# Gated products cut into pieces of 293 columns, differences moved to GpSimd, weight sums and end loads moved in a fused attention and gated feed-forward kernel

## The chip, the cores and the metric

One core of one Trainium2 chip runs the whole program. Its engines are TensorE (PE: matmuls; its weight loads are listed as PEld), VectorE (DVE), ScalarE (ACT), GpSimd (POOL) and SyncE (SP, which here only issues DMAs). The metric is the device time of one execution in microseconds (us); smaller is better.

## The reference, cut to what matters

```python
# x: 2048 x 512, 32 heads of 16, F = 1792
g = sigmoid((x * gate_w).sum(-1, keepdims=True))
q, k, v = heads of x @ wqkv
a = softmax(q @ k.T / 4) @ v  @ wo                     # attention
b = (sigmoid(x @ w_gate) * (x @ w_up)) @ w_down        # gated linear unit
out = g * a + (1 - g) * b
```

## The kernel before, in words

**Main loop.** 256 periods, two steps of 128 keys by 1024 queries each. A period holds 8 score matmuls (L679), each followed by an exponential on ScalarE (L681); 8 matmuls whose largest values a later pair of heads needs (L293), each followed by a maximum over its 512 columns on VectorE (L295, "reduce" below); 12 groups of dense matmuls (L164: gate, up and later query and key weights, in high and low halves); and 16 value matmuls (L953). The period is named by the number k in `values(k)`, and V is the start of its value matmuls. The strings `STEADY` (periods 0 to 244) and `LAST` (from 245, without reduces) are the order on TensorE.

**What sets the order of the rest.** `plans(k, kind, step)` puts a step into period k: "load" steps at its start (DMAs on SP's queue), "pool" steps into the list `later`, "act" steps before `values(k)`, "dve" steps right behind it, which is behind the period's 8th reduce. `work` lets GpSimd work off the lists, for about 2 us in mid period and 2.6 us at its end. In mid period GpSimd also passes a token (`turn`, L175) that TensorE's next dense group waits for. GpSimd's standing work is the dense products' partial sums (L541: `chain`, `had`, `side`), a sum of value products per period (L970) and the splits of weights into halves (L138, L141).

**Gated products.** `plan_quad(i, c, k0)` takes four 128 x 512 tiles of gate (`hg`) and up (`hu`), makes tanh on ScalarE (L725), `(tanh + 1) * up` on VectorE (`gated`, L737) and four differences T1 to T4 (`minus`, L740), and stores seven tiles in `op_d`. A quad takes 8 periods, and there are 13; the 14th is `last_quad` in the end. Before, k0 is 139 + 16i + 8c; the four whole-tile products fall in periods k0 + 3, 5, 7, 10, T1 and T2 on VectorE in k0 + 6 and 8, T3 and T4 on GpSimd in k0 + 10 and 11.

**Weight sums and denominators.** `plan_combos` forms sums of blocks of `w_down` on GpSimd (four additions of 128 x 256 each) for seven f. `denominators` loads softmax sums as 32 rows of 512, takes the reciprocal in pieces on VectorE (L910), multiplies by the gate (L912) and stores them in `rec_d`.

**End.** 98 units of six matmuls (two halves, seven products `PRODUCTS`, seven f; L1252) use a stored tile `op`, split by ScalarE (L103) and VectorE (L106), with up to nine tiles loaded ahead (L875); between them come 132 matmuls of the attention output (L151), whose inputs `heads_split` multiplies by the denominators (L1142), and the weights of later products (`weights_at`).

Of the kernel before, what the change touches and what calls it, by code (L numbers as in the profile page):

```python
# [45 lines left out]
def gated_mix(ctx, tc, x, xT, wqk, wv, wo, w_gate, w_up, w_down, gate_w, out):  # L46
# [28 lines left out]
    g_d = dram.tile([2, NS, 4, 32], F32, name="g_d")  # L75
    wc_d = dram.tile([2, HF, P, 2, 256], F32, name="wc_d")
# [13 lines left out]
    den = keep.tile([P, 512], F32, name="den")  # L90
# [645 lines left out]
    def gated(j, g, u):  # L736
        dve.scalar_tensor_tensor(u[j], g[j], 1.0, u[j], op0=ALU.add, op1=ALU.mult)  # L737
# [5 lines left out]
    T1, T2, T3, T4 = (1, 1, 0), (1, 2, 1), (0, 1, 0), (2, 3, 1)  # L743

    def plan_quad(i, c, k0):
        u, g = [None] * 4, [None] * 4

        def load(a, j):
            f, ci = quad(i, c)[j]
            to = (g, u)[a]  # L750
            to[j] = keep.tile([P, 512], F32, name=f"h{'gu'[a]}{i}{c}{j}", tag="hu" if a else "hg", bufs=6 if a else 2)
# [83 lines left out]
    plans(134, "load", lambda: g1_rows(0))  # L835
# [4 lines left out]
    homes = {"A11": cells(1), "S2": cells(3), "S1": cells(0), "S4": cells(2)}  # L840
# [25 lines left out]
    wider = {name: wide_cells(c) for name, c in (("A11", 1), ("S2", 3), ("S1", 0), ("S4", 2))}  # L866
# [4 lines left out]
    def op_load(m):  # L871
        if m < len(seq):
            half, n, f = seq[m]
            raws[m] = keep.tile([P, 512], F32, name=f"op{m}", tag="hu", bufs=6)
            sp.dma_start(raws[m], op_d[half, n, f])  # L875

    def op_split(m, engine=act):
# [8 lines left out]
        split(h, l, raws.pop(m), engine, dve)  # L886
        ops[m] = h, l

    def plan_weights(n, name, f0):
# [5 lines left out]
        plans(NPER - 10 + n, "load", load)  # L895
        plans(NPER - 9 + n, "dve", lambda: weight_split(name, raw[0], f0, dve, dve))

    for n, (name, f0) in enumerate((name, f0) for name in ("A11", "S2") for f0 in range(0, HF, 2)):
        plan_weights(n, name, f0)
# [81 lines left out]
    dens = [denominators(i, r0, r0 + 32, n) for r0, i, n in ((0, 0, 8), (0, 1, 8), (32, 0, 4), (32, 1, 8))]  # L981
    plans(NPER - 10, "load", lambda: g1_rows(32))
    for n, ks in enumerate(([*range(122, 131), 141], [*range(130, 139), 143], [249, 251, 252, 253, 254, 255])):
        for k in ks:
            plans(k, "dve", lambda n=n: next(dens[n], None))
# [70 lines left out]
    for m in range(4, 9):  # L1056
# [4 lines left out]
    late = {}  # L1061

    def late_tiles():
# [5 lines left out]
        for name in ("S3", "A12", "A22"):  # L1069
            hl = [a22[:, a] for a in range(2)] if name == "A22" else [big(f"{name}{t}", F32R) for t in "hl"]  # L1070
            homes[name] = [[t[:, f * 256:(f + 1) * 256] for t in hl] for f in range(HF)]
            wider[name] = {f: [t[:, f * 256:(f + 2) * 256] for t in hl] for f in range(0, HF - 1, 2)}
# [19 lines left out]
    def last_quad(i, c):  # L1092
# [4 lines left out]
        def load(j):  # L1097
            f, ci = quad(i, c)[j]
            g[j] = keep.tile([P, 512], F32, name=f"hgl{j}", tag="hg", bufs=2)
# [5 lines left out]
        for j in range(4):  # L1105
            hid_tanh(g[j])
# [186 lines left out]
```

## Time and profile before

| | us |
|---|---|
| median of 3 runs (lowest, highest) | 1742.25 (1740.31, 1743.64) |
| profiled execution | 1739.23 |
| its span | 1737.4 |
| TensorE busy in the span | 1698.2 |
| VectorE, ScalarE, GpSimd busy | 1549.0, 1408.3, 1042.1 |

Read the profile by stretch: periods 0 to 138 up to 876 us, the gated products from there to 1486 us, the `LAST` order to 1535 us, the end to 1737 us. TensorE counts as busy nearly everywhere, but an entry of a busy TensorE can hide a matmul that takes longer than its own work, so period lengths (from V to V) say more than busy shares. An undisturbed period takes 5.575 us.

### The profile page before, as it was taken

To read this page: it belongs to the slowest core of one execution; us is meant where nothing else is said; L and a number is where in the kernel's file an instruction comes from. 1 tells how busy PE (TensorE), PEld (TensorE's weight loads), DVE (VectorE), ACT (ScalarE), POOL (GpSimd) and SP (SyncE) were. 2 spreads that over 40 slices of the span, in tenths; PEclk is the share of its full clock that TensorE was granted. 3 is DMA by queue.
4 is the path that set the end of the run, shared out by engine and by line. 5 is a ranking of instruction groups with operands and counts; after the bars stand their busy time and mean duration, and the time that the engine had idled before them with its cause. 6 is when DMAs were issued, how large, how long until landed. Compare 5 with 4: busy or idle time off the path is not lost.

```text
span 1737.4 us, 35521 instructions
## 1 busy us (share of the span) xinstructions
PE 1698.2 (98%) x12401; PEld 1039.0 (60%) x12401; DVE 1549.0 (89%) x2499; ACT 1408.3 (81%) x2818; POOL 1042.1 (60%) x1007
## 2 busy tenths in 40 slices
PE   9999999999999999999999999999999999987988
PEld 7756655656565566555555555555555555455767
DVE  7988888878889999999999999999999999688764
ACT  4288888978888898888899999999999998964331
POOL 1033567656766666666667777777777767446403
PEclk9999999999999999999999999999999999999999
DMA  7512455484656464557456675767685767468883
GB/s 247 161 45 71 131 188 174 161 267 166 195 166 184 145 180 142 145 175 205 127 158 208 179 217 178 217 186 209 196 224 184 200 206 231 147 204 259 283 248 123
DMA packets 180533, 318.40 MB, mean 183 GB/s; under 512 B 29120, under 2 KB 42560, under 8 KB 177472
## 3 DMA queue, kind: packets, MB, share of 16 engines
q1 hardware_dynamic: 172736, 301.43, 57.5%
q10 hardware_dynamic: 7616, 14.68, 2.7%
q8 instruction: 98, 1.61, 0.4%
q14 instruction: 83, 0.68, 0.2%
HBM read 184.16 MB, written 131.87 MB: 182 GB/s over the span
## 4 chain that ended last, share of the span: by engine, by line
PE 76%; DVE 10%; DMA 5%; ACT 5%; issue 2%; POOL 1%; SPq 0%; DVEq 0%; ACTq 0%; POOLq 0%
PE dn L164 24%; PE sm L953 23%; PE sm L293 14%; DVE stat L295 6%; PE sm L679 4%; PE st L679 4%; ACT p L681 3%; DMA op<-op_d 2%; PE st L293 2%; PE st L643 1%; PE st L151 1%; DVE ops L106 1%; PE sm L1252 1%; DVE hu L737 1%; DMA hpl<-hp_d 1%
## 5 line engine op out<-in xcount | busy, mean ns | idle before, releaser
L295 DVE TENSOR_REDUCE stat<-sm 128x1 f32<-128x512 f32 x1313 | 847.0, 680 | 95.0 <-PE sm L679 82.2
L681 ACT ACTIVATE p<-sm 128x512 f32<-128x512 f32 x1027 | 612.7, 622 | 12.6 <-PE sm L679 8.9
L681 ACT ACTIVATE p<-st 128x512 f32<-128x512 f32 x1019 | 609.0, 641 | 1.5 <-PE st L679 1.4
L293 PE MATMUL sm<-ks,qs 48*128 48x512 f32 x1313 | 523.8, 436 | 3.3 <-DVE stat L295 2.1
L953 PE MATMUL sm<-p,v 128*17 128x512 f32 x4016 | 480.9, 596 | 0.0
L295 DVE TENSOR_REDUCE stat<-st 128x1 f32<-128x512 f32 x735 | 479.1, 679 | 0.2 <-PE st L293 0.2
L679 PE MATMUL sm<-qs,ks 64*128 64x512 f32 x1027 | 428.6, 420 | 5.4 <-ACT p L681 5.2
L679 PE MATMUL st<-qs,ks 64*128 64x512 f32 x1019 | 426.8, 420 | 0.0
L293 PEld LDWEIGHTS sm<-ks,qs 48*128 48x128 f32 x1313 | 239.6, 184 | 283.0 <-DVE stat L295 237.0
L970 POOL TENSOR_TENSOR sum<-sum,part 128x512 f32<-128x512 f32 x224 | 289.9, 1294 | 136.5 <-PE sm L679 101.3
L293 PE MATMUL st<-ks,qs 48*128 48x512 f32 x735 | 290.7, 395 | 0.0
L953 PEld LDWEIGHTS sm<-p,v 128*17 128x17 f32 x4016 | 93.1, 97 | 232.2 <-issue 157.8
L958 ACT ACTIVATE part<-sm 128x512 f32<-128x512 f32 x214 | 128.1, 599 | 117.0 <-issue 69.2
L679 PEld LDWEIGHTS st<-qs,ks 64*128 64x128 f32 x1019 | 187.9, 184 | 33.7 <-issue 3.4
L541 POOL TENSOR_TENSOR chain<-chain,chain 128x512 f32<-128x512 f32 x96 | 124.0, 1291 | 128.2 <-ACT p L681 47.1
L679 PEld LDWEIGHTS sm<-qs,ks 64*128 64x128 f32 x1027 | 189.7, 185 | 16.7 <-ACT p L681 7.6
L541 POOL TENSOR_TENSOR had<-chain,had 128x512 f32<-128x512 f32 x96 | 123.8, 1290 | 42.0 <-PE sm L679 23.9
L293 PEld LDWEIGHTS st<-ks,qs 48*128 48x128 f32 x735 | 137.3, 187 | 1.5 <-ACT p L681 0.6
L103 ACT ACTIVATE ops<-op 128x512 fp32r<-128x512 f32 x94 | 55.7, 624 | 66.4 <-DMA op<-op_d 34.2
L106 DVE TENSOR_TENSOR ops<-op,ops 128x512 fp32r<-128x512 f32 x94 | 84.4, 931 | 27.6 <-ACT ops L103 27.4
L607 ACT ACTIVATE chain<-dn 128x512 f32<-128x512 f32 x128 | 85.4, 667 | 0.0
L541 POOL TENSOR_TENSOR side<-side,side 128x512 f32<-128x512 f32 x32 | 41.3, 1292 | 69.6 <-PE sm L679 68.3
(871 smaller groups left out, 3334.4 us busy)
## 6 DMA issues: line engine op xcount, KB each, us to landing
op<-op_d SPq DMA_DIRECT2D x98, 256.0 KB
op_d<-hu SPq DMA_DIRECT2D x91, 256.0 KB
had<-gu_d SPq DMA_DIRECT2D x84, 256.0 KB
gu_d<-had SPq DMA_DIRECT2D x84, 256.0 KB
gu_d<-side SPq DMA_DIRECT2D x56, 256.0 KB
hg<-gu_d SPq DMA_DIRECT2D x52, 256.0 KB
hu<-gu_d SPq DMA_DIRECT2D x52, 256.0 KB
pv_d<-sum SPq DMA_DIRECT2D x32, 256.0 KB
```

What stands on the lines that cost most here:

```text
L103: act.activation(h, src, AF.Copy)
L106: return lo.tensor_tensor(l, src, h.bitcast(F32), ALU.subtract)
L164: mm = pe.matmul(self.o, a[rows], b[rows], start=(self.n == 0), stop=(self.n == 2 * len(self.ops) - 1))
L293: pe.matmul(t, qs[r:r + KM, qt * P:(qt + 1) * P], ks[r:r + KM, g * 512:(g + 1) * 512], start=True, stop=True)
L295: dve.tensor_reduce(stat[half][:, b, qt % 8, g:g + 1], t, axis=AX.X, op=ALU.max)
L541: pool.tensor_tensor(to, u, w, ALU.add)
L607: leave = lambda e, o: act.activation(e, o, AF.Copy)
L679: pe.matmul(o, ks[r:r + KR, (kt + a) * P:(kt + a + 1) * P], qs[r:r + KR, q0:q0 + 512], start=True, stop=True)
L681: act.activation(pt[:, 2 * a + c, :], o, AF.Exp, scale=DH ** -0.5)
L953: pe.matmul(o[32 * c:32 * c + VW, :], v[:, 2 * k % 16 + a, h * VW:(h + 1) * VW], pts[c // 2][:, 2 * a + c % 2, :], start=(a == 0), stop=(a ...
L958: act.activation(e, o, AF.Copy)
L970: pool.tensor_tensor(s, s, e, ALU.add)
```

## The change

- Gated products are cut into seven pieces of 293 columns, in periods k0 + 1 to k0 + 7 with k0 = 140 + 16i + 8c. Where a piece crosses the edge of a 512 column tile, it is two instructions: 219 + 74, 145 + 148 and 71 + 222 columns; the last has 290. That is 10 instructions for 4. All four differences run on GpSimd. T1 needs tiles 1 and 0, T2 tiles 2 and 1, T4 tile 3 and T2, T3 T2 and tile 0. Loads start two periods earlier, and `hg` has 3 buffers for 2.
- `plan_combos`: two additions in each of two periods, (8, 10), (14, 17), (18, 23), (30, 35), (42, 43), (46, 47), (50, 51), for four additions in 42, 46, 49, 51, 61, 69, 73.
- Denominators: tiles of 128 x 64, one reciprocal and one product each, in 135 to 138, 245, 246, 251 and in the end, for 28 pieces on 32 rows in 122 to 143, 249 to 255 and the end.
- Last periods: the weights S3 are loaded and split there too (two splits a period instead of one); `op` tiles 0 to 3 a period earlier; tiles 4 to 11 into free places of `xh` and `xl`, and 12 and 13; four units of heads are multiplied by the denominators on GpSimd (`plan_unit`) and stored in `on_d`.
- End: `wo` is loaded at its start; S3's splits there are gone; `op` tiles are loaded one further ahead; `last_quad` spreads over 37 to 53.

```diff
+    PIECE = 293
+    T1, T2, T3, T4 = (1, 1, 0), (2, 2, 1), (0, 2, 0), (1, 3, 2)
...
         def sub(k, step, n):
             def run():
+                minus(pool, u, *step)
                 plans(now[0] + 1, "load", lambda: hid_out(c, n, i, u[step[0]]))
+            plans(k0 + k, "pool", lambda: later.append((1.3, run)))
...
+        for n in range(7):
+            for j in range(4):
+                cols = slice(max(PIECE * n, 512 * j) - 512 * j, min(PIECE * (n + 1), 512 * (j + 1)) - 512 * j)
+                if cols.start < cols.stop:
+                    plans(k0 + 1 + n, "dve", lambda j=j, cols=cols: gated(j, g, u, cols))
...
+        sub(7, T1, 3)
+        sub(9, T2, 4)
+        sub(9, T4, 2)
+        sub(10, T3, 6)
...
-            plan_quad(i, c, 139 + 16 * i + 8 * c)
+            plan_quad(i, c, 140 + 16 * i + 8 * c)
...
-    for f, k in enumerate((42, 46, 49, 51, 61, 69, 73)):
+    for f, k in enumerate(((8, 10), (14, 17), (18, 23), (30, 35), (42, 43), (46, 47), (50, 51))):
...
+    for n, (name, f0) in enumerate((name, f0) for name in ("A11", "S2", "S3") for f0 in range(0, HF, 2)):
+        plan_weights(NPER - 11 + n // 2, name, f0)
     for m in range(4):
-        plans(NPER - 5 + m, "load", lambda m=m: op_load(m))
+        plans(NPER - 6 + m, "load", lambda m=m: op_load(m))
         plans(NPER - 4 + m, "dve", lambda m=m: op_split(m, dve))
...
+        plans(NPER - 4 + m // 2, "load", lambda m=m: op_load(m + 4))
+    for m in range(8, 14):
+        plans(NPER - 2 + m // 12, "load", lambda m=m: op_load(m))
...
+    for i, k, at in ((0, 0, 134), (1, 0, 135), (0, 1, 136), (1, 1, 137), (0, 2, 244), (1, 2, 245), (0, 3, 250)):
+        plan_den(i, k, at)
...
+    PRE = [(2, 0), (2, 1), (2, 2), (0, 2)]
...
+        def run():
+            pool.tensor_tensor(t[0][:, 0], t[0][:, 0], t[0][:, 1], ALU.mult)
+            plans(now[0] + 1, "load", lambda: sp.dma_start(on_d[n], t[0][:, 0]))
...
+    for n in range(4):
+        plan_unit(n, 247 + 2 * n)
...
-    weights_at("S3", (0, 4), (0, 7))
...
-                    op_load(m + f + 9)
+                    op_load(max(17, m + f + 10))
```

**First place, the gated products.** VectorE before, around T1 of one quad, in period 169 (`hu111` is tile 1 of quad i = 1, c = 1; `stat` a reduce):

```order
L295 TENSOR_REDUCE stat11_0_12515<-st1_66 128x1
L295 TENSOR_REDUCE stat11_0_12515<-sm2_71 128x1
L295 TENSOR_REDUCE stat11_0_12515<-sm3_72 128x1
L740 TENSOR_TENSOR hu111_12586<-hu111_12586,hu110_12436 128x512
L295 TENSOR_REDUCE stat11_0_12515<-sm3_72 128x1
L295 TENSOR_REDUCE stat11_0_12515<-st0_65 128x1
```

One whole difference or product stood behind every 8 reduces. VectorE after, in the second of the quad's periods, where its two pieces cross from tile 0 to tile 1:

```order
L296 TENSOR_REDUCE stat11_0_12535<-st1_66 128x1
L296 TENSOR_REDUCE stat11_0_12535<-sm2_71 128x1
L296 TENSOR_REDUCE stat11_0_12535<-sm3_72 128x1
L738 SCALAR_TENSOR_TENSOR hu110_12384<-hg110_12314,hu110_12384 128x219
L738 SCALAR_TENSOR_TENSOR hu111_12533<-hg111_12455,hu111_12533 128x74
L296 TENSOR_REDUCE stat11_0_12535<-sm3_72 128x1
L296 TENSOR_REDUCE stat11_0_12535<-st0_65 128x1
```

Now two pieces stand in a row, and the differences are gone from this engine. GpSimd before, around period 165's end (T3 and T4 of the quad before are `hu100` and `hu102`; `part165` marks the period):

```order
L740 TENSOR_TENSOR hu100_11852<-hu101_12002,hu100_11852 128x512
L541 TENSOR_TENSOR chain02_11_12566<-chain02_11_12566,chain02_10_12492 128x512
L541 TENSOR_TENSOR had02_10_12421<-chain02_11_12566,had02_10_12421 128x512
L970 TENSOR_TENSOR sum10_0_12225<-sum10_0_12225,part165_12580 128x512
L740 TENSOR_TENSOR hu102_12144<-hu103_12299,hu101_12002 128x512
L541 TENSOR_TENSOR chain02_12_12639<-chain02_12_12639,chain02_11_12566 128x512
L541 TENSOR_TENSOR had02_12_12568<-chain02_12_12639,had02_12_12568 128x512
L970 TENSOR_TENSOR sum10_0_12225<-sum10_0_12225,part166_12651 128x512
```

A difference stood in each of two periods. GpSimd after, at the same place (`cb` is the low half of a weight):

```order
L741 TENSOR_TENSOR hu102_12083<-hu102_12083,hu101_11943 128x512
L741 TENSOR_TENSOR hu101_11943<-hu103_12243,hu102_12083 128x512
L542 TENSOR_TENSOR chain02_11_12585<-chain02_11_12585,chain02_10_12510 128x512
L542 TENSOR_TENSOR had02_10_12438<-chain02_11_12585,had02_10_12438 128x512
L1034 TENSOR_TENSOR sum10_0_12239<-sum10_0_12239,part165_12600 128x512
L741 TENSOR_TENSOR hu100_11794<-hu102_12083,hu100_11794 128x512
L139 TENSOR_TENSOR cb(1, 2)l_12226<-chain1_9r_12142,cb(1, 2)h_12225 128x512
L542 TENSOR_TENSOR chain02_12_12655<-chain02_12_12655,chain02_11_12585 128x512
L542 TENSOR_TENSOR had02_12_12587<-chain02_12_12655,had02_12_12587 128x512
L1034 TENSOR_TENSOR sum10_0_12239<-sum10_0_12239,part166_12669 128x512
```

T2 moved in beside T4, T3 came a period later, and the weight's low half moved behind T3.

**Second place, the head of the output (`of`) at period 239.** TensorE's dense groups wait for `xh` and `xl` of `of1`. GpSimd before, from the low half `xl` of the part before:

```order
L138 TENSOR_TENSOR xl_111<-of0_17799,xh_110 128x2x256
L740 TENSOR_TENSOR hu510_17076<-hu511_17226,hu510_17076 128x512
L541 TENSOR_TENSOR chain16_11_17795<-chain16_11_17795,chain16_10_17721 128x512
L541 TENSOR_TENSOR had16_10_17634<-chain16_11_17795,had16_10_17634 128x512
L970 TENSOR_TENSOR sum14_1_17440<-sum14_1_17440,part237_17811 128x512
L562 TENSOR_TENSOR of1_17870<-xh_110,xl_111 128x512
L141 CAST xh_110<-of1_17870 128x2x256
L138 TENSOR_TENSOR xl_111<-of1_17870,xh_110 128x2x256
```

One difference stood ahead of `of1`. GpSimd after, from the same operation:

```order
L139 TENSOR_TENSOR xl_112<-of0_17873,xh_111 128x2x256
L741 TENSOR_TENSOR hu512_17361<-hu512_17361,hu511_17221 128x512
L741 TENSOR_TENSOR hu511_17221<-hu513_17513,hu512_17361 128x512
L542 TENSOR_TENSOR chain16_11_17869<-chain16_11_17869,chain16_10_17794 128x512
L542 TENSOR_TENSOR had16_10_17706<-chain16_11_17869,had16_10_17706 128x512
L1034 TENSOR_TENSOR sum14_1_17509<-sum14_1_17509,part237_17885 128x512
L563 TENSOR_TENSOR of1_17941<-xh_111,xl_112 128x512
L142 CAST xh_111<-of1_17941 128x2x256
L139 TENSOR_TENSOR xl_112<-of1_17941,xh_111 128x2x256
```

Two differences stand there now.

**Third place, SP and ScalarE near 370 us.** On SP, `wc` are weight sums, `side` and `had` partial sums, `chain2` weights; DMAHW0 to 7 are the semaphores that DMAs take in turn, and a DMA waits for the last one on its own. SP before:

```order
L502 DMA s_d_83<-side20_10_4482 128x512 [waits DMAHW3_49,Activation_49]
L796 DMA wc_d_80<-wc20_4142 128x512 [waits DMAHW5_49]
L796 DMA wc_d_80<-wc21_4144 128x512 [waits DMAHW6_49]
L110 DMA chain2_2r_4551<-in_wqk_dram 128x2x256 [waits DMAHW7_49]
L110 DMA chain2_3r_4553<-in_wqk_dram 128x2x256 [waits DMAHW0_49]
L525 DMA had20_00_4838<-s_d_83 128x512 [waits DMAHW2_49,DMAHW1_49]
L796 DMA wc_d_80<-wc30_4284 128x512 [waits Pool_49]
L796 DMA wc_d_80<-wc31_4286 128x512 [waits DMAHW3_49,Pool_49]
L525 DMA had20_02_4977<-s_d_83 128x512 [waits DMAHW4_49]
```

Two stores of sums (`wc20`, `wc21`) stood ahead of the loads of `chain2`. SP after:

```order
L503 DMA s_d_84<-side20_10_4515 128x512 [waits DMAHW1_49,Activation_49]
L111 DMA chain2_2r_4584<-in_wqk_dram 128x2x256 [waits DMAHW2_49]
L111 DMA chain2_3r_4586<-in_wqk_dram 128x2x256 [waits DMAHW4_49]
L526 DMA had20_00_4869<-s_d_84 128x512 [waits DMAHW7_49,DMAHW5_49]
L526 DMA had20_02_5008<-s_d_84 128x512 [waits DMAHW6_49]
L798 DMA wc_d_81<-wc60_4246 128x512 [waits Pool_49]
L798 DMA wc_d_81<-wc61_4248 128x512 [waits DMAHW0_49,Pool_49]
```

Those stores are gone. ScalarE before, with the loads of `xh` and `xl` of the next dense part:

```order
L681 ACTIVATE p52_1_4526<-st0_65 128x512 [waits PE_49]
L607 ACTIVATE side20_11_4547<-dn_68 128x512 [waits DMAHW7_49,PE_49]
L375 DMA xh_110<-t_d_82 128x2x512 [waits DMAHW6_49]
L375 DMA xl_111<-t_d_82 128x2x512 [waits DMAHW1_49]
L958 ACTIVATE part51_4567<-sm0_69 128x512 [waits DVE_49,PE_49,Pool_49]
```

`xl` waited for DMAHW1, which `had20_00` held. ScalarE after:

```order
L682 ACTIVATE p52_1_4559<-st0_65 128x512 [waits PE_49]
L608 ACTIVATE side20_11_4580<-dn_68 128x512 [waits DMAHW6_49,PE_49]
L376 DMA xh_111<-t_d_83 128x2x512 [waits DMAHW1_49]
L376 DMA xl_112<-t_d_83 128x2x512 [waits DMAHW2_49]
L1022 ACTIVATE part51_4598<-sm0_69 128x512 [waits DVE_49,PE_49,Pool_49]
```

It waits for DMAHW2 now, which `chain2_2r` held.

## Rows read from the trace of the kernel before

**Rows 1.** Busy us by stretch: PE, PEld, DVE, ACT, POOL; clock; DMA share; GB/s.

```profile
899.30:1462.90 563.60, 560.83 (x4273) 319.69 (x4276) 549.30 (x875) 520.42 (x1068) 415.16 (x365) 1.00 0.68 201
1485.90:1534.70 48.80, 45.69 (x334) 20.88 (x332) 33.95 (x46) 45.00 (x92) 22.99 (x21) 1.00 0.39 127
1534.70:1600.00 65.30, 52.84 (x222) 37.81 (x222) 55.03 (x65) 32.91 (x59) 34.21 (x23) 1.00 0.79 249
1600.00:1680.00 80.00, 72.38 (x298) 56.33 (x298) 52.83 (x74) 30.23 (x53) 26.26 (x19) 0.98 0.87 273
1680.00:1737.40 57.40, 51.34 (x208) 40.55 (x206) 31.66 (x44) 12.59 (x22) 16.43 (x12) 0.94 0.48 150
```

**Rows 2.** TensorE's timeline (start, duration): V of periods 139, 151, 164, 165, 239, 244.

```profile
876.59 1.90 PE L953 MATMUL sm<-p,v 128*17 128x512 f32 x14
...
946.06 1.48 PE L953 MATMUL sm<-p,v 128*17 128x512 f32 x12
...
1021.47 0.62 PE L953 MATMUL sm<-p,v 128*17 128x512 f32 x4
...
1027.05 0.62 PE L953 MATMUL sm<-p,v 128*17 128x512 f32 x4
...
1455.30 1.05 PE L953 MATMUL sm<-p,v 128*17 128x512 f32 x8
...
1485.94 0.62 PE L953 MATMUL sm<-p,v 128*17 128x512 f32 x4
```

**Rows 3.** VectorE's timeline in periods 166, 167; in brackets idle time ahead, releaser.

```profile
1034.49 1.10 DVE L737 SCALAR_TENSOR_TENSOR hu<-hg,hu 128x512 f32<-128x512 f32 x1
1035.51 0.68 DVE L295 TENSOR_REDUCE stat<-sm 128x1 f32<-128x512 f32 x1
...
1041.08 0.69 DVE L295 TENSOR_REDUCE stat<-sm 128x1 f32<-128x512 f32 x1 [0.70 <-PE sm L679]
```

**Rows 4.** GpSimd's timeline in period 166.

```profile
1033.76 1.28 POOL L970 TENSOR_TENSOR sum<-sum,part 128x512 f32<-128x512 f32 x1
1034.98 1.75 POOL L740 TENSOR_TENSOR hu<-hu,hu 128x512 f32<-128x512 f32 x1
```

**Rows 5.** VectorE's timeline at 1476 us, a product with GpSimd quiet.

```profile
1476.39 0.68 DVE L737 SCALAR_TENSOR_TENSOR hu<-hg,hu 128x512 f32<-128x512 f32 x1
```

**Rows 6.** Timelines of VectorE and of GpSimd at 1527 us.

```profile
1526.82 0.43 DVE L105 CAST xh<-wfS 128x512 fp32r<-128x512 f32 x1
1527.28 1.66 DVE L106 TENSOR_TENSOR xl<-wfS,xh 128x512 fp32r<-128x512 f32 x1
...
1526.93 1.45 POOL L970 TENSOR_TENSOR sum<-sum,part 128x512 f32<-128x512 f32 x1 [2.86 <-DVE part L960]
```

**Rows 7.** Timelines of GpSimd and of TensorE at period 239.

```profile
1456.73 1.27 POOL L138 TENSOR_TENSOR xl<-of,xh 128x512 fp32r<-128x512 f32 x1
...
1458.05 0.50 PE L164 MATMUL dn<-xl,wo0h 64*128 64x512 f32 x1 [0.17 <-POOL xl L138]
```

**Rows 8.** Timelines of ScalarE and of TensorE near 379 us.

```profile
379.05 0.37 ACTq L375 DMA_DIRECT2D xl<-t_d  x1
...
380.68 0.79 PE L679 MATMUL sm<-qs,ks 64*128 64x512 f32 x1 [2.92 <-ACT p L681]
```

**Rows 9.** VectorE's timeline in period 130: gate copies, a denominator's piece.

```profile
826.00 0.72 DVE L813 COPY mpad<-g 128x16 f32<-128x16 f32 x1
...
826.97 0.50 DVE L910 RECIPROCAL den<-den 32x64 f32<-32x64 f32 x1
```

**Rows 10.** Groups by line, GpSimd: additions of the weight sums (count, busy us, mean ns).

```profile
L793 POOL TENSOR_TENSOR wc<-wc,wc 128x256 f32<-128x256 f32 x21 | 15.4, 736 | 2.2 <-PE sm L679 0.6 <-DMA s_d<-had 0.6
```

**Rows 11.** Timeline of TensorE in period 246.

```profile
1498.21 0.50 PE L164 MATMUL dn<-xh,wo0h 64*128 64x512 f32 x1 [1.26 <-POOLq L175]
```

**Rows 12.** The end: waits from 1534.7 to 1680 us (us, times, longest); a chain step.

```profile
ACT ops L103 <- DMA op<-op_d: 28.9, 16, 3.4
...
1576.90 8.45 DMA op<-op_d
```

More of the change, by code (lines that the diff above doesn't have):

```diff
@@ L89, in gated_mix @@
     mpad = turns(mpads)
-    den = keep.tile([P, 512], F32, name="den")
+    g1q = keep.tile([P, 2, 64], F32, name="g1q")
     logit = keep.tile([P, NS], F32, name="logit")
@@ L894, in load, with big_home @@
             weight_load(name, raw[0], f0)
[L895 to L899, printed above, removed]
+        plans(k, "load", load)
+        plans(k + 1, "dve", lambda: weight_split(name, raw[0], f0, dve, dve))
+    def big_home(name, tiles=None):
+        hl = tiles or [big(f"{name}{t}", F32R) for t in "hl"]
+        homes[name] = [[t[:, f * 256:(f + 1) * 256] for t in hl] for f in range(HF)]
+        wider[name] = {f: [t[:, f * 256:(f + 2) * 256] for t in hl] for f in range(0, HF - 1, 2)}
@@ new lines, in gated_mix, with unit_sources, plan_unit, load @@
+    PRE = [(2, 0), (2, 1), (2, 2), (0, 2)]
+    def unit_sources(c, k):
+        i, q = divmod(c, 2)
+        heads = pv_d[i].rearrange("p (b c r) q -> (p b) c r q", b=2, c=2)
+        recs = rec_d.rearrange("(i h c) q -> i h c q", i=2, c=2)
+        hs = slice(8 * k, 8 * k + 8)
+        return heads[hs, q, :DH, :], recs[i, hs, q, :].unsqueeze(1).to_broadcast([8, DH, 512])
+    def plan_unit(n, at):
+        t = []
+        def load():
+            t.append(keep.tile([P, 2, 512], F32, name=f"on{n}", tag="ev", bufs=2))
+            for a, src in enumerate(unit_sources(*PRE[n])):
+                sp.dma_start(t[0][:, a], src)
+        def run():
+            pool.tensor_tensor(t[0][:, 0], t[0][:, 0], t[0][:, 1], ALU.mult)
+            plans(now[0] + 1, "load", lambda: sp.dma_start(on_d[n], t[0][:, 0]))
+        plans(at, "load", load)
+        plans(at + 1, "pool", lambda: later.append((1.3, run)))
@@ L979, in mx @@
                 yield
[L981 to L985, printed above, removed]
     run = next(fill)
@@ L1055, in gated_mix @@
     flush(later)
-    for m in range(4, 9):
+    for k in (0, 2):
+        wo_load(k)
+    for m in range(14, 18):
         op_load(m)
@@ L1068, in late_tiles @@
         late["g0"] = [rest[:, :512], rest[:, :512], rest[:, 512:], rest[:, 512:]]
[L1069 to L1072, printed above, removed]
+        big_home("S4")
+        big_home("A22", [a22[:, a] for a in range(2)])
     def g0_load(*cs):
@@ L1098, in load @@
             f, ci = quad(i, c)[j]
[L1099 removed]
+            g[j] = keep.tile([P, 512], F32, name=f"hgl{j}", tag="hg", bufs=3)
             hid_load(0, f, ci, g[j])
```

172 lines of the change are left out of this document (89 added, 83 removed).

## The prediction, made before the changed kernel had run

> **What bounds the kernel now.** I read busy time by stretch first. From 899 to 1463 us TensorE is busy 560.83 of 563.60 us, but VectorE 549.30 too [rows 1], so either may be late. Next the V of each period, the start of its value matmuls. A period in which nothing is late takes 5.58 us (1021.47 to 1027.05) [rows 2]; I use 5.575. Between V139 at 876.59 and V151 at 946.06 there are 12 periods, 66.90 us, and 2.57 are lost; from there to V239 at 1455.30 there are 88, 490.60, and 18.64 are lost, 1.69 in each of 11 quads of 8 periods; the five periods to V244 lose 2.77 [rows 2]. That is 23.98 us, the stretch of the gated products.
>
> VectorE's timeline tells why. Behind a clean period's 8th reduce it idles 0.70 us for a matmul [rows 3], so with the overlap of 0.08 to 0.09 between entries (1034.49 + 1.10 against 1035.51) about 0.79 us is free. A product alone takes 0.68 [rows 5] and would fit. In period 166 it takes 1.10, and the next reduce starts 1.02 later [rows 3]: 0.23 lost. GpSimd's sum runs there from 1033.76 to 1035.04 [rows 4], and the product, begun at 1034.49, ends 0.55 behind that. Then GpSimd's next operation, a difference that takes 1.28 when alone, takes 1.75 [rows 4]: it was held up by the product in turn. At 1527 us the same is seen with two VectorE instructions in a row: the cast ends, GpSimd's sum, which had been started behind it, takes 1.45, and the second VectorE instruction takes 1.66, until 0.56 behind GpSimd's end [rows 6]. So each waits for the whole of the other's operation, and they alternate. Reduces keep their 0.68 [rows 3] whatever GpSimd does.
>
> From 1534.7 us on TensorE is idle 12.5 of 65.3 us, then 7.6 of 80.0 and 6.1 of 57.4, where its clock is also below full (0.94) [rows 1]. ScalarE's splits wait 28.9 us for loads of `op`, and the chain has one such load of 8.45 us [rows 12], while the transfer engines are 0.79 to 0.87 busy [rows 1].
>
> **Gated products, cycles.** Before: 1.69 lost a quad. After, a piece of 293 columns alone: it begins with GpSimd's sum in flight, as in period 166, waits 0.55 (1035.04 less 1034.49) [rows 3, 4], and then needs 293/512 of 0.55, 0.31. That is 0.86, and 0.07 is lost; three such periods a quad lose some 0.14 together. A pair of pieces is another matter. The first ends, GpSimd's waiting fourth operation goes ahead, as the sum does in [rows 6], and the second piece waits for all of it. By the order, the fourth operation is a sum (about 1.15 after its start) in the period of 219 + 74, an addition of 256 columns (0.74 as in [rows 10], of which I count 0.6) in that of 145 + 148, and a cast (0.61, counted 0.5) in that of 71 + 222. So the first pair takes 0.55 + 0.24 + 1.15 + 0.08 = 2.02, and 1.2 is lost; the second 0.55 + 0.16 + 0.6 + 0.16 = 1.47, 0.68 lost; the third 0.55 + 0.08 + 0.5 + 0.24 = 1.37, 0.58 lost; I take 0.6 for both. With 0.1 for the write of the maxima, which now stands ahead of a sum, a quad loses 1.2 + 1.2 + 0.14 + 0.11 = 2.65. That is 0.96 more, 11 times: **+10.5**. Two differences more on GpSimd cost nothing of their own: its 415 busy us of 564 [rows 1] leave room; without it each would add its 1.28, 28 us over 11 quads. Bounds: 0.6 a quad if no second piece waits (-12), and 4 if a full sum of 1.15 stands between all three pairs (+25). I take the value from the order, since [rows 6] shows the alternation itself.
>
> [...]
>
> **Gated products, edges.** The first quad's pairs find no differences of an earlier quad on GpSimd; I put 0.5 for it where 2.57 was lost: **-2.1**. The last quad's pairs fall into periods 238 to 242, where GpSimd also adds and splits the head of the output: **+1.1**. At period 239 `xl` of `of1` ends at 1458.00 and TensorE had waited 0.17 for it [rows 7]. In the new order two differences stand ahead of `of1` where one stood. They add two operations of 1.27 to a queue that had no slack; `xl` then comes some 3.1 us late and is met with 0.3 more in period 240, 3.4 to 3.5 where 2.77 was lost: **+0.8**. Bounds for the three: -2.5 to +3. The stretch in all: **+10.3**.
>
> **Weight sums.** In the quiet first periods two additions of 0.74 [rows 10] fit, but in period 23, where by the order the other operations are 5.0 us at their durations here, GpSimd comes to 6.5 us, above 5.575, and its token for TensorE is late: **+0.6**, between 0 and 1.1. Near 379 us it pays back. TensorE idles 2.92 there, since ScalarE stood behind its DMA of `xl`, issued only at 379.05 [rows 8]; with the slow clock behind it, periods 48 to 70 lose 7.5. The issue waits for the semaphore that the load of `had` holds, which stood on SP's queue behind two stores of sums. In the new order it waits for `chain2_2r` instead, two rows earlier, and those two stores are gone: **-5**, between 0, if another DMA is late, and -5.7. What stays is a second, smaller stall near 472 us, which no moved edit touches.
>
> **Denominators.** A piece alone (0.50) fits into the 0.79. Behind a gate copy it begins at 826.97, 0.97 after that [rows 9], when the 0.79 are over, and its 0.50 less the overlap of 0.08 is lost whole. Four periods (126 and 130 to 132) have a piece behind another operation: **-1.7**. The four new reciprocals with a product of 64 columns come in 135 to 138, alone, and may lose up to 0.4 each: between -2.5 and 0.
>
> **Last periods.** VectorE is busy 33.95 of 48.8 us and GpSimd 22.99 [rows 1], but what alternates adds up: by the order, VectorE's splits, products and GpSimd's work come to some 39.4 us in 245 to 254 after, 30 before, in 38.4 us. In 246 TensorE waits 1.26 for GpSimd's token [rows 11], and in 245 to 247 the sum grows from 12.8 to 16 us in 11.5. Two splits of weights a period, four products of heads: **+3**, from 0, if all hides beside ScalarE's 45.00 of 48.8 [rows 1], to +9, if all of the growth shows.
>
> **The end.** S3's splits (0.9 MB loaded), ten `op` tiles (2.6 MB), `wo` (1 MB) and a part of the denominators (1 MB) leave the stretch in which the loads are late: 5.5 MB, some 22 us of transfer at 249 GB/s [rows 1]. Of the 12.5 us that TensorE idles until 1600 [rows 1] nearly all hangs on loads of `op`, denominators and `wo` in turn (8.45 is one link of the chain [rows 12]); I take 12 of them and 1.5 of what comes behind: **-13.5**. Bounds: -3, if VectorE (55.03 of 65.3 [rows 1]) is the next to be late, and -20, with the idle time to 1680.
>
> **The sum.** 0.6 - 5 - 1.7 + 10.3 + 3 - 13.5 = -6.3. The profiled execution took 1739.23 us, with a span of 1737.4; 1733 follows for it. The median of the runs, 1742.25, is 3.0 above it, so for the median I say **1736**. A difference under 0.2%, 3.5 us, can't be told from none.
>
> **Rivals.** (1) *The loads aren't what the end waits for.* If behind the loads VectorE's splits and GpSimd's additions, which wait for each other as above, hold TensorE up, the end gains 3, not 13.5, and the loop's loss stands: 1736 + 10.5 = 1746.5, slower. For it: VectorE's 55.03 of 65.3 in that stretch [rows 1]. Against: 28.9 us of waits for `op` loads [rows 12], and seven splits of S3 and 12 reciprocals leave VectorE or GpSimd there. It decides where the end gains less than about 4 us. (2) *The stall near 379 us stays*, since another DMA holds the semaphore: 1736 + 5 = 1741, no change. For it: a load that is late through a full queue is late under any name, and 5 wide loads of `w_down` stood in the queue. Against: they move away with the sums. (3) *No second piece waits*, since GpSimd doesn't get in between two VectorE instructions so short: a quad loses 0.6, 22.5 us less over 11: 1713.5. Against: [rows 6]. (4) The change may not do what it says, if pieces and differences were ordered otherwise; the order shows them as told, so I give it nothing.
>
> **How the numbers follow.** The forecast 0.45 (its own range 1730 to 1741), rival 1 0.25, rival 2 0.22, rival 3 0.08. The range goes from 1724, the forecast with the end at -20 and a little of the cycles' lower bound, to 1749, rival 1 with a little of the last periods' +9; it leaves out rival 3 and the ends of the others. Faster by over 0.2%: the forecast and rival 3, 0.53; within 0.2%: rival 2, 0.22; slower: rival 1, 0.25.
>
> **What would show it.** In the changed profile: V to V over the 88 periods gives 490.6 + 11 x 2.65 = 520; a second piece of 74 columns that takes over 1 us, in the shadow of a GpSimd sum; a TensorE idle entry of some 3 us for `xl` near period 239; no 2.92 us entry near 379 us; one reciprocal at a time in 135 to 138 without a late reduce; waits of ScalarE for `op` under 15 us until 1680, and TensorE idle under 3 us in the first 65 us of the end. If short second pieces don't wait, or if the end idles as much as before, the prediction is wrong by 10 to 22 us, and in which direction is told by which of the two it is.

## The result, and the profile after

The changed kernel takes 1746.9 us (median of 9 runs, 1743.06 to 1750.63), the kernel before 1741.83 beside it (9 runs): ratio 1.0033, 95% interval 1.0019 to 1.0047. It is slower by about a third of a percent; a gain of as much had been foretold. The profiled execution's span is 1743.5 us where it was 1737.4, so the two traces differ by 6.1, like the medians (5.1), and can be set beside each other stretch by stretch, from V to V:

| stretch | before, us | after, us | difference | foretold |
|---|---|---|---|---|
| start to V48 | 357.3 | 359.2 | +1.9 | +0.6 |
| V48 to V70 | 130.1 | 124.2 | -5.9 | -5 |
| V70 to V139 | 389.2 | 387.0 | -2.1 | -1.7 |
| V139 to V151 | 69.5 | 69.1 | -0.4 | -2.1 |
| V151 to V239 | 509.2 | 522.0 | +12.8 | +10.5 |
| V239 to V244 | 30.6 | 31.7 | +1.1 | +1.9 |
| V244 to V255 | 48.8 | 59.6 | **+10.9** | **+3** |
| V255 to the end | 202.7 | 190.6 | -12.1 | -13.5 |

Seven terms came out within 2.5 us of what was foretold. The last periods did not: they lost 10.9 us, above even the bound of 9 put on them. That alone turns the sum from a gain of 6.3 into a loss of 1.6.

The V's of the changed kernel, TensorE's timeline (start, duration), answer to [rows 2], for periods 139, 151, 239, 244 and 255:

```profile
870.41 0.62 PE L1017 MATMUL sm<-p,v 128*17 128x512 f32 x4
...
939.46 0.62 PE L1017 MATMUL sm<-p,v 128*17 128x512 f32 x4
...
1461.50 0.62 PE L1017 MATMUL sm<-p,v 128*17 128x512 f32 x4
...
1493.24 0.62 PE L1017 MATMUL sm<-p,v 128*17 128x512 f32 x4
...
1552.86 0.62 PE L1017 MATMUL st<-p,v 128*17 128x512 f32 x4
```

The busy times of its last periods and of its end, by stretch as in [rows 1]:

```profile
1493.24:1552.86 59.62, 49.50 (x334) 22.62 (x333) 39.72 (x58) 45.29 (x90) 30.78 (x25) 0.94 0.59 195
1552.86:1743.50 190.64, 170.63 (x725) 132.69 (x724) 126.78 (x165) 73.19 (x130) 71.53 (x49) 0.99 0.70 224
```

TensorE idled 3.1 of 48.8 us in the last periods before [rows 1], and 10.1 of 59.6 now; VectorE has 6 us more to do there, and the granted clock is 0.94 where it was 1.00. In the end TensorE idles 20.0 of 190.6 us; before it was 26 (12.5 + 7.6 + 6.1 of [rows 1]). The prediction named two signs for the end. In the changed kernel these are the row of its first 65 us, and ScalarE's waits for loads of `op` from its start to 1698 us:

```profile
1552.91:1618.00 65.09, 60.99 (x270) 47.27 (x269) 50.67 (x59) 34.53 (x63) 37.18 (x25) 1.00 0.74 241
...
ACT ops L104 <- DMA op<-op_d: 32.7, 18, 5.3
```

TensorE idles 4.1 us there, where 12.5 were measured before and under 3 foretold. But ScalarE's waits did not shrink: 32.7 us where they had been 28.9 [rows 12] and under 15 was foretold.

**A pair of pieces.** VectorE and then GpSimd in period 166 of the changed kernel, the period of [rows 3] and [rows 4]:

```profile
1029.66 0.86 DVE L738 SCALAR_TENSOR_TENSOR hu<-hg,hu 128x219 f32<-128x219 f32 x1
...
1030.44 1.32 DVE L738 SCALAR_TENSOR_TENSOR hu<-hg,hu 128x74 f32<-128x74 f32 x1
1031.68 0.68 DVE L296 TENSOR_REDUCE stat<-sm 128x1 f32<-128x512 f32 x1
...
1029.00 1.27 POOL L542 TENSOR_TENSOR had<-chain,had 128x512 f32<-128x512 f32 x1
1030.24 1.43 POOL L1034 TENSOR_TENSOR sum<-sum,part 128x512 f32<-128x512 f32 x1
```

The first piece waits for `had` (until 1030.27) and ends at 1030.52. The sum was started at 1030.24 and ends at 1031.67, and the piece of 74 columns, a seventh of a tile, ends 0.09 behind that. It takes 1.32 us, nearly all of it waiting. The next reduce starts 2.02 after the first piece; 2.02 less the free 0.79 is 1.23 lost, where 1.2 was foretold.

**The last periods.** VectorE, GpSimd and TensorE in period 247, with two splits of weights A11 in a row:

```profile
1506.33 0.83 DVE L106 CAST xh<-wfA 128x512 fp32r<-128x512 f32 x1
1507.19 1.67 DVE L107 TENSOR_TENSOR xl<-wfA,xh 128x512 fp32r<-128x512 f32 x1
1508.78 0.54 DVE L939 RECIPROCAL den<-den 128x64 f32<-128x64 f32 x1
1509.36 0.71 DVE L940 TENSOR_TENSOR den<-den,g1q 128x64 f32<-128x64 f32 x1
1509.99 0.68 DVE L1024 COPY part<-st 128x512 f32<-128x512 f32 x1
...
1506.95 1.36 POOL L139 TENSOR_TENSOR xl<-of,xh 128x512 fp32r<-128x512 f32 x1
1508.26 1.72 POOL L741 TENSOR_TENSOR hu<-hu,hu 128x512 f32<-128x512 f32 x1
...
1510.72 0.50 PE L680 MATMUL st<-qs,ks 64*128 64x512 f32 x1 [2.17 <-DVE part L1024]
```

TensorE needs a score bank that `part`'s copy (L1024) frees. That copy stands on VectorE behind the splits, and the splits and GpSimd's operations alternate: 1.67 and 1.72 for what takes 0.69 and 1.28 alone. So far this is the wait that was priced. At 1531 us it is another one:

```profile
1531.43 0.43 DVE L106 CAST S3h<-wfS 128x512 fp32r<-128x512 f32 x1 [4.25 <-DMA wfS<-wc_d]
...
1534.30 0.50 PE L680 MATMUL sm<-qs,ks 64*128 64x512 f32 x1 [2.20 <-DVE part L1024]
```

Here VectorE does nothing for 4.25 us but wait for a weight, and the next copy is held up behind it. A slower clock follows both stalls in this trace. In each of these two windows of five microseconds the granted clock is 0.66 (0.50 from 1517 to 1519 and from 1541 to 1543; estimated from the 0.66, some 3.4 us at 0.50 in each), the first after TensorE had idled 2.17 and 1.87 us at 1510.7 and 1515.6, the second after 2.20 and 2.38 us at 1534.3 and 1539.7; in the other eight from 1500 to 1550 it is 1.00:

```profile
1515.00:1520.00 5.00, 4.42 (x25) 2.20 (x29) 3.28 (x6) 3.53 (x7) 0.00 (x0) 0.66 0.81 265
...
1540.00:1545.00 5.00, 5.00 (x31) 2.05 (x27) 1.25 (x3) 3.54 (x7) 1.47 (x1) 0.66 0.86 300
```

### The profile page after: what moved, and what is told of

Same layout as the page of the kernel before. It is cut to its first block, busy times and chain, and to the rows that moved or that the text cites. A ratio compares the mean times of both kernels' runs of the same rounds, so it can differ in the third digit from the quotient of the medians.

```text
span 1743.5 us, 35585 instructions
## 1 busy us (share of the span) xinstructions
PE 1690.8 (97%) x12401; PEld 1038.6 (60%) x12401; DVE 1554.6 (89%) x2539; ACT 1404.6 (81%) x2814; POOL 1071.2 (61%) x1033
## 4 chain that ended last, share of the span: by engine, by line
PE 61%; DVE 19%; DMA 10%; issue 3%; POOL 3%; ACT 3%; SPq 1%; DVEq 0%; POOLq 0%; ACTq 0%
PE dn L165 19%; PE sm L1017 18%; DVE stat L296 12%; PE sm L294 11%; DVE hu L738 4%; PE st L680 3%; PE sm L680 3%; DMA op<-op_d 2%; PE st L294 2%; ACT p L682 2%; DMA had<-gu_d 2%; DVE ops L107 1%; DMA max_d<-mhl 1%; PE st L644 1%; PE st L152 1%
## 5 line engine op out<-in xcount | busy, mean ns | idle before, releaser
L294 PE MATMUL sm<-ks,qs 48*128 48x512 f32 x1313 | 522.4, 435 | 17.9 <-DVE stat L296 17.6
L738 DVE SCALAR_TENSOR_TENSOR hu<-hg,hu 128x293 f32<-128x293 f32 (+7 forms) x130 | 105.5, 834 | 0.0
L107 DVE TENSOR_TENSOR ops<-op,ops 128x512 fp32r<-128x512 f32 x86 | 73.2, 887 | 31.8 <-ACT ops L104 31.6
L104 ACT ACTIVATE ops<-op 128x512 fp32r<-128x512 f32 x86 | 50.9, 624 | 59.3 <-DMA op<-op_d 34.7
L741 POOL TENSOR_TENSOR hu<-hu,hu 128x512 f32<-128x512 f32 x52 | 70.5, 1356 | 35.8 <-PE sm L680 19.6
```

The source lines that it names most:

```text
L107: return lo.tensor_tensor(l, src, h.bitcast(F32), ALU.subtract)
L294: pe.matmul(t, qs[r:r + KM, qt * P:(qt + 1) * P], ks[r:r + KM, g * 512:(g + 1) * 512], start=True, stop=True)
L738: dve.scalar_tensor_tensor(u[j][:, cols], g[j][:, cols], 1.0, u[j][:, cols], op0=ALU.add, op1=ALU.mult)
L741: engine.tensor_tensor(u[to], u[a], u[b], ALU.subtract)
```

## The experiments

All kernels but where it is said are the changed kernel with one edit. Stretches are from each kernel's one profiled execution. How far one execution can be trusted is told by kernels that share a stretch's code: the end takes 189.0 to 194.3 us in the changed kernel, e1, e4, e5, e6 and e10, and V244 to V255 57.2 to 59.6 in the changed kernel, e1, e5 and e10. So differences under some 5 us in the end, and under some 2.5 in the last periods, are not told apart by two traces.

| kernel | median, us | ratio to before (interval) | V151 to V239 | V244 to V255 | end |
|---|---|---|---|---|---|
| before | 1741.83 | 1 | 509.2 | 48.8 | 202.7 |
| changed | 1746.9 | 1.0033 (1.0019, 1.0047) | 522.0 | 59.6 | 190.6 |
| e1_whole_tiles | 1719.7 | 0.9878 (0.9856, 0.9900) | 502.8 | 58.3 | 189.0 |
| e10_halves_twice | 1743.9 | 1.0016 (1.0003, 1.0030) | 522.4 | 57.2 | 191.8 |
| e4_ring | 1743.0 | 1.0012 (0.9999, 1.0024) | 521.8 | 55.0 | 191.9 |
| e2_no_units | 1743.2 | 1.0011 (0.9997, 1.0025) | 522.7 | 56.3 | 190.2 |
| e3_s3_end | 1743.5 | 1.0011 (0.9997, 1.0025) | 522.4 | 53.0 | 197.9 |
| e8_op_ring | 1745.1 | 1.0018 (1.0003, 1.0032) | 522.7 | 58.8 | 194.6 |
| e6_tiles_ring | 1716.2 | 0.9856 (0.9840, 0.9872) | 499.2 | 56.5 | 192.4 |
| e9_tiles_ring_no_units | 1712.9 | 0.9836 (0.9816, 0.9855) | 503.2 | 51.7 | 194.4 |
| e11_spread | 1708.7 | 0.9813 (0.9794, 0.9832) | 499.8 | 49.8 | 190.1 |

**Is it the pair? e1_whole_tiles.**

```diff
-    PIECE = 293
+    PIECES = [(0, 0, 256), (0, 256, 512), (1, 0, 256), (1, 256, 512), (2, 0, 256), (2, 256, 512), (3, 0, 512)]
...
+        for n, (j, c0, c1) in enumerate(PIECES):
+            plans(k0 + 1 + n, "dve", lambda j=j, cols=slice(c0, c1): gated(j, g, u, cols))
```

> The changed kernel, but no piece crosses a tile: the seven pieces are halves of 256 columns of tiles 0, 1 and 2 and the whole of tile 3, one instruction a period, everything else as it is. Theory (the second piece of a pair waits for a GpSimd operation that goes ahead between the two): a quad loses about 0.8 us (six halves 0.05 to 0.1, one 0.4 where GpSimd runs late, the whole tile 0.23) where 2.86 are lost now, 11 quads: about 22 us less, 1724 us, and below the kernel before. Rival (four differences on GpSimd are what costs, by load or by a late token): at least 2.3 a quad stay, 1741 us or more.

V151 to V239 take 502.8 us: 12.2 lost over 11 quads, 1.1 a quad, where the changed kernel loses 2.86 and the kernel before 1.69. Of these 12.2, 3.8 fall in period 238, where TensorE idles 2.67 us for a load (`qs<-max_d`). Counted over eleven whole quads, V148 to V236, e1 loses 0.76 a quad, close to the 0.8 expected, the changed kernel 2.80 and the kernel before 1.69. The whole falls to 1719.7, below the kernel before. V of periods 151 and 239, and a single piece with GpSimd in flight, the next reduce 0.82 after it:

```profile
937.64 0.62 PE L1014 MATMUL sm<-p,v 128*17 128x512 f32 x4
...
1440.39 1.05 PE L1014 MATMUL sm<-p,v 128*17 128x512 f32 x4
...
1024.96 0.90 DVE L738 SCALAR_TENSOR_TENSOR hu<-hg,hu 128x256 f32<-128x256 f32 x1
1025.78 0.68 DVE L296 TENSOR_REDUCE stat<-sm 128x1 f32<-128x512 f32 x1
```

The rival, four differences on GpSimd, falls: they are all still there, on the same engine in the same periods.

**Two instructions, or the edge of a tile? e10_halves_twice.** From e1, three halves are cut once more, each into two instructions of 128 columns of one tile; columns per period stay.

```diff
+    PIECES = [(0, 0, 0, 256), (1, 0, 256, 384), (1, 0, 384, 512), (2, 1, 0, 256), (3, 1, 256, 384), (3, 1, 384, 512),
+              (4, 2, 0, 256), (5, 2, 256, 384), (5, 2, 384, 512), (6, 3, 0, 512)]
```

> The pieces that cross no tile, but in three of the seven periods (the same three that hold a pair in the changed kernel) the half of 256 columns is two instructions of 128 columns of the same tile. The columns a period are unchanged. Theory (GpSimd's waiting operation goes ahead between two VectorE instructions): such a period loses 0.5 to 1.3 us, a quad 3.2 to 3.5 in all where 1.1 are lost with single pieces: 24 us more over 11 quads, 1744 us. Rival (it is the crossing to the next tile that waits, for its tanh or load, or 10 to 11 fixed costs of an instruction, 0.1 each): within 4 us of the single pieces' 1720.

The loss is back, to the microsecond: 522.4 us in the 88 periods, 1743.9 in all, 24 us above e1 (eleven whole quads: 2.85 lost in each). VectorE's two instructions and GpSimd's sum of one such period:

```profile
1028.33 0.77 DVE L738 SCALAR_TENSOR_TENSOR hu<-hg,hu 128x128 f32<-128x128 f32 x1
...
1029.02 1.37 DVE L738 SCALAR_TENSOR_TENSOR hu<-hg,hu 128x128 f32<-128x128 f32 x1
...
1028.90 1.34 POOL L1032 TENSOR_TENSOR sum<-sum,part 128x512 f32<-128x512 f32 x1
```

The two are of one tile and one size; the first ends behind the operation in flight, the second behind the sum. So it is the second instruction that costs, not the crossing.

**Loads or alternation in the last periods? e4_ring and e2_no_units.** The edit of e4_ring:

```diff
-            raw.append(keep.tile([P, min(2, HF - f0), 256], F32, name=f"wf{name}{f0}", tag="wr", bufs=2))
+            raw.append(keep.tile([P, min(2, HF - f0), 256], F32, name=f"wf{name}{f0}", tag=tag, bufs={"wr": 2, "hg": 3}[tag]))
...
-        plan_weights(NPER - 11 + n // 2, name, f0)
+        plan_weights(NPER - 11 + n // 2, name, f0, ("wr", "hg")[n % 2])
```

> The changed kernel, where every second raw weight of the last periods takes a buffer of the gate tiles (three, free by then) in place of one of its own two, so a load doesn't wait for the split just ahead of it. VectorE's work is unchanged. Theory L (load after split after load): periods 244 to 255 become 5 to 6 us shorter, 1741 us. Theory K (VectorE and GpSimd alternate): under 1.5 us shorter, 1746 us.

The last periods went from 59.6 to 55.0 us, and the wait for S3's first half is all but gone on VectorE's timeline:

```profile
1527.97 0.43 DVE L106 CAST S3h<-wfS 128x512 fp32r<-128x512 f32 x1 [0.30 <-DMA wfS<-wc_d]
```

VectorE's work is the same, so this is theory L's cost: two loads a period in two buffers. It is 4.6 us between these two traces; against the 57.2 of e10, with the same last periods as the changed kernel, it would be 2.2. The medians differ by 3.9. A load has to wait for the period's splits, which are its last VectorE work, and then has less than a period of 3.83 us to land; in the changed kernel the load for S3's first half is issued at 1525.44, and its cast begins at 1531.43.

The edit of e2_no_units:

```diff
-    PRE = [(2, 0), (2, 1), (2, 2), (0, 2)]
+    PRE = []
```

> The changed kernel without the four head units multiplied on GpSimd in the last periods; they are multiplied in the end, as before. Theory K (VectorE and GpSimd wait for each other in the last periods): periods 244 to 255, 59.6 us now, become about 5 us shorter. Theory L (a weight's load waits for the split that frees its buffer, and the next split waits for the load): not more than 2 us shorter. The end gets up to 2 us longer by either.

3.3 us less in the last periods, between what K and L said, and by the spread of the traces not far from none; the medians differ by 3.7. The end is as long as with the units done ahead (190.2 and 190.6). The stall of 2.17 us in period 247 stays in both e2 and e4, as it must: no load and no unit takes part in it.

**Do they add? e6_tiles_ring and e9_tiles_ring_no_units.** e1 with e4's edit, and with e2's too.

> Pieces that cross no tile, and every second raw weight in a gate buffer. If the two don't touch each other, the last periods lose the 4.6 us that the buffers alone took from them: 58.3 to 53.7 us, and 1715 in all.

The median fell by 3.5 us from e1; in its one trace the last periods took 56.5, 1.8 less than e1's. 4.6 had been expected. The size of the buffers' gain is thus known to some 3 us only.

> Pieces that cross no tile, every second raw weight in a gate buffer, and no head units on GpSimd in the last periods. If waits for loads (4.6 us) and alternation with the units (3.3 us) are separate costs, periods 244 to 255 take 58.3 - 7.9 = 50.5 us, near the 48.8 of the kernel before, and the whole 1712. If both stand behind the same late splits, they don't add: 53 to 54 us and 1715.

51.7 us in the last periods, 6.6 less than e1; 7.9 were expected if the two costs are separate, 4 to 5 if not. The median is 3.3 below e6's. They mostly add. V of periods 244 and 255:

```profile
1468.33 0.62 PE L1014 MATMUL sm<-p,v 128*17 128x512 f32 x4
...
1519.99 0.63 PE L1014 MATMUL st<-p,v 128*17 128x512 f32 x4
```

**The rest of it: e11_spread.** From e9, one weight a period in 246 to 248, two from 249 on.

```diff
-        plan_weights(NPER - 11 + n // 2, name, f0)
+        plan_weights(NPER - 11 + (0, 1, 2, 3, 3, 4, 4, 5, 5, 6, 6, 7)[n], name, f0, ("wr", "hg")[n % 2])
```

> Single pieces, the wider buffers, no head units, and the weights' splits one a period in 246 to 248, two a period from 249 on. If what is left of the last periods' loss is two splits a period beside GpSimd's work on the head of the output (246 and 247), periods 246 to 248, 10.9 us, go to 9.4 and the last periods to 50.2; 1711 us. If the later periods lose what the early ones gain, 1713.

V246 to V248 went from 10.9 to 8.0 us, period 248 from 6.1 to 3.9, and the last periods to 49.8, 1 us above the kernel before, with S3 still split there. Period 252 took 8.0 where e9 has 5.1. One idle entry of TensorE is left, in that period, 2.6 us at 1502, behind a weight that lands late:

```profile
1499.44 0.43 DVE L106 CAST S3h<-wfS 128x512 fp32r<-128x512 f32 x1 [2.82 <-DMA wfS<-wc_d]
```

At 1708.7 us, 1.9% below the kernel before (interval 1.7 to 2.1%), it is the best of the kernels.

**What did the end gain by? e3_s3_end and e8_op_ring.** The first puts S3 and `wo` back into the end:

```diff
-    for n, (name, f0) in enumerate((name, f0) for name in ("A11", "S2", "S3") for f0 in range(0, HF, 2)):
+    for n, (name, f0) in enumerate((name, f0) for name in ("A11", "S2") for f0 in range(0, HF, 2)):
...
-    for k in (0, 2):
-        wo_load(k)
...
+    weights_at("S3", (0, 4), (0, 7))
+    for k, (load, use) in zip((0, 2), ((11, 16), (13, 18))):
+        step_at(load, lambda k=k: wo_load(k))
```

> The changed kernel with S3's weights loaded and split in the end, as before, and wo loaded there at units 11 and 16; the last periods keep two loads and two splits a period for the other two weights. Both theories: the last periods 252 to 254 lose their late splits, some 4 to 5 us less; 247 and 248 keep theirs. The end gets longer by S3's share of what it gained, 3 to 6 us: 1745 to 1749 in all. If S3's share of the end is under 2 us, it isn't S3 that the end gained by, and the time is 1742 to 1744.

The end takes 197.9 us, 7.3 more, and the last periods 53.0, 6.6 less. In the whole end TensorE idles 26.2 us before, 24.5 in e3 and 20.0 in the changed kernel (18.2 to 20.9 in all others). So S3 and `wo` early are the larger part of the idle time that the end gained, and S3 cost nearly as much in the last periods. Whether it is their loads or S3's splits on VectorE and GpSimd that the end was rid of, this run does not tell: both went back.

The second lets the ten `op` tiles be loaded as before:

```diff
-        if 4 <= m < 12:
+        if m < 0:
...
-    for m in range(14, 18):
+    for m in range(4, 9):
...
-                    op_load(max(17, m + f + 10))
+                    op_load(m + f + 9)
```

> The changed kernel with the op tiles from 4 on in their own six buffers alone, loaded as before (from the start of the end, nine ahead), while S3, wo, the denominators and the four units stay early. Theory (the end gained by all its early loads): the end, 190.6 us now, gets 3 to 5 us longer, since S3 and wo alone gave 7.4 of its 12; the last periods up to 1 us shorter. If the end stays within 1.5 us, these ten tiles gave nothing and S3 and wo were it all.

194.6 us, 3.9 more in its one trace; but e9, with the tiles early, has 194.4, and the intervals of the ratios (1.0018 and 1.0033) overlap. The 3.9 us are not idle time: TensorE idles 18.2 us in that end and 20.0 in the changed kernel, while the granted clock is 0.95 there and 0.99 here. No run shows a gain from the ten tiles.

**The stall near 379 us: e5_old_sums.**

```diff
-    for f, k in enumerate(((8, 10), (14, 17), (18, 23), (30, 35), (42, 43), (46, 47), (50, 51))):
+    for f, k in enumerate(((42, 42), (46, 46), (49, 49), (51, 51), (61, 61), (69, 69), (73, 73))):
```

> The changed kernel with the weight sums back at one period each (42, 46, 49, 51, 61, 69, 73). Theory (the stall near 379 us came from the sums' stores ahead of other DMAs): from V48 to V70, 124.2 us now, back to about 130; before V48 1.4 us less; the rest as it is. Rival (the stall went for another reason, such as loads and buffers of the other changes, or depends on the run): 124 stays.

V48 to V70 take 129.3 us again (130.1 before, 124.2 changed), and the stretch ahead is 1.5 shorter. The idle entry of TensorE is back, with ScalarE's DMA issue ahead of it, as in [rows 8]:

```profile
379.30 0.37 ACTq L376 DMA_DIRECT2D xl<-t_d  x1
...
380.93 0.49 PE L680 MATMUL sm<-qs,ks 64*128 64x512 f32 x1 [2.81 <-ACT p L682]
```

The changed kernel's entry at that place:

```profile
380.06 0.50 PE L680 MATMUL sm<-qs,ks 64*128 64x512 f32 x1 [0.43 <-ACT p L682]
```

So the sums did it; the other kernels, all with the new sums, take 123.6 to 124.4 there. Period 67, at the second stall near 472 us, loses 1.7 here, 1.8 before and 0.3 in the changed kernel, so the sums took most of that one too. This kernel's one run took 1755.2 us, with a granted clock of 0.989 over the span where the changed kernel's profile has 0.997. 5.8 us of the excess lie in V151 to V239, which this edit doesn't touch, and stay unexplained.

## Why the prediction was wrong

**The step that failed is "last periods: +3, from 0 to +9".** They cost 10.9 (8.4 to 10.9 in the four kernels with that code). The step added up what alternates on VectorE and GpSimd, 39.4 us in 38.4, and took a few us of it to show. Two things were missing. First, a load: the sum priced the second split of a period as VectorE time alone, though its raw tile comes through two buffers, so load and split now follow each other in a ring. e4_ring shows it: 4.6 us in its trace, 3.9 in the median. Second, a total hides the period that is over. The prediction saw 245 to 247 at 16 us in 11.5 and let most of it hide. But in period 247 two splits, a denominator and GpSimd's `of`, its two halves and a difference alternate, and the copies that TensorE waits for stand behind all of them: 247 and 248 lost 5.8 us, where the kernel before lost 1.7, in 246. e11_spread, which moves loads and splits away from there, got 5.1 us back in periods 246 to 248, of which 2.9 were lost again in 252. The units on GpSimd were 3.3 (e2_no_units; 3.7 in the median). Each size is known to some 2 us only. Both longer stalls were then followed by some 3.4 us at a granted clock of 0.50, which no term had.

**The end: right in size, its reason shown in part.** It gained 12.1 for 13.5 foretold (8.4 to 13.7 in the six kernels that share its code). Rival 1, which let it win 3, is refuted, although its total (1746.5) is nearly the measured one: it comes from another place. Of the 12.1, 6.2 are idle time of TensorE; the rest is busy time, 176.5 us before and 170.6 after, at a granted clock of 0.97 and 0.99, for which the prediction had no term. By idle time, e3_s3_end puts 4.5 of the 6.2 down to S3 and `wo`; the ten `op` tiles, 2.6 of the 5.5 MB that the term counted, show nothing (e8_op_ring). And ScalarE's waits for `op` loads, on which the argument leaned, grew from 28.9 to 32.7 us. So that the loads' 22 us of transfer were what the end waited for is not shown.

**The quads: right in kind, 2.3 short.** The first two pairs lose 1.2 and 0.59 as foretold (1.23 and 6.16 - 5.575). By e1 and e10, rival 3 (no second piece waits) falls. The third pair loses 0.6 or less in six of the eleven quads only; in the other five it loses 0.7 to 1.4, which the order of one quad could not tell. In four of these five GpSimd waits for a load of `had`, so its sum, not the short cast, stands between the pieces (GpSimd, then VectorE, period 178 of the changed kernel):

```profile
1100.42 1.28 POOL L542 TENSOR_TENSOR had<-chain,had 128x512 f32<-128x512 f32 x1 [1.47 <-DMA had<-gu_d]
1101.66 1.29 POOL L1034 TENSOR_TENSOR sum<-sum,part 128x512 f32<-128x512 f32 x1
...
1100.90 2.29 DVE L738 SCALAR_TENSOR_TENSOR hu<-hg,hu 128x71 f32<-128x71 f32 x2
```

Of the 2.3, 0.7 are not of the quads: period 238, which holds a first pair, lost 1.93, and the head of the output stands there too. In V148 to V236 a quad loses 2.80 where 2.65 was foretold.

**The edges: 2.57 lost in the first quad before, 2.15 after, where 0.5 was foretold.** The three pairs of the first quad lose 0.2, 0.2 and 0.15 (periods 142, 144 and 146), the little that was said. But the stretch to V151 also holds the first pair of the next quad, in period 150, with 1.25 (a period of 6.82), which the prediction left out. Near period 239 TensorE did wait for `xh` and `xl`, as said, but less:

```profile
1464.66 0.50 PE L165 MATMUL dn<-xh,wo0h 64*128 64x512 f32 x1 [0.58 <-POOL xh L142]
1466.01 0.49 PE L165 MATMUL dn<-xl,wo0h 64*128 64x512 f32 x1 [0.85 <-POOL xl L139]
```

That is 1.43 where some 3 were expected, since two differences had begun in the period before, in which GpSimd was free (the two from 1454.23 to 1457.11, then 1.46 us idle). Periods 238 to 240 together lose 5.0 us, 3.0 before.

**The quiet periods: right, with one error.** V48 to V70 gained 5.9 for 5, shown by e5: 4.7 at the stall near 379 us, and 1.5 at the one near 472, which the prediction said no moved edit touches. V70 to V139 gained 2.1 for 1.7, which no run took apart; in the traces periods 126 and 130 to 132 lose 2.0 us less, and 135 to 137 lose nothing. Up to V48 1.9 us were lost for 0.6: 0.3 in period 23 (5.86) and 0.3 in 38, in every kernel with the new sums and not in e5; 0.8 in 36, which is 0 to 0.8 in kernels with the same code there; and 0.6 ahead of V0, where no sum stands. The other periods of the sums, 42, 43, 46 and 47 among them, lose nothing.

## What to carry to other kernels

An instruction cut in two so that each half fits into a gap did not fit here where two pieces stood in one gap with GpSimd at work: the second product on VectorE waited for the GpSimd operation between the two (1.32 us for 74 columns, with a sum of 1.43; 1.37 for 128, with one of 1.34), so cut where no period gets two. When work is moved into a stretch that looks idle, price the ring of buffers it comes through, load by load, and the fullest period, not the mean of ten. And when one sum has terms of both signs, the error to look for is in the term with the least traced ground under it; here that was one of the small ones.

## What the runs showed that was not expected

A VectorE cast with one input waited for GpSimd too: 0.43 us with GpSimd idle (at 1531.43 above), 0.83 with a GpSimd operation in flight (at 1506.33) and, on a tile of half the columns, up to 1.36, where it takes 0.28 with GpSimd idle:

```profile
1513.11 1.36 DVE L106 CAST xh<-wfA 128x256 fp32r<-128x256 f32 x1
...
1525.24 0.28 DVE L106 CAST xh<-wfS 128x256 fp32r<-128x256 f32 x1
```

The first of the two ends at 1514.47, 0.15 behind a GpSimd product that ran from 1512.60 to 1514.32. The prediction named only the second, two-input instruction of a split as one that waits.

The time between two VectorE instructions was enough for GpSimd to take its turn: in e10_halves_twice, with 256 columns cut into twice 128, the next reduce starts 1.99 us after the first piece (1028.33 to 1030.32), where it starts 0.82 after the single piece of e1, so the cut cost 1.2 us there and added no columns.
